# Another order and bank table behind chunk 0's first results in an attention-and-expert kernel

## The chip, the cores and the metric

The kernel runs on one core of one Trainium2 chip. The metric is the device time of one execution in microseconds; the time before is the median of three runs. A profile of one more execution shows what each engine did: TensorE (PE, with its weight loads as PEld), VectorE (DVE), ScalarE (ACT), GpSimd (POOL), SyncE (SP, which only issues DMAs here) and the 16 DMA engines.

## What is computed

```python
# attention: 8 batches, 8 heads, 576 positions, head size 64
kv  = einsum('bhsd,bhse->bhde', k, v)
out = einsum('bhsd,bhde->bhse', q, kv)
rms = sqrt(mean(out * out, axis=-1) + 1e-06)
x   = out / rms * g_norm                  # to 4608 tokens x 512
# expert layer: 512 -> 1024 -> 512
h    = x @ w_in
solu = h * softmax(h)
ln   = (solu - mean(solu)) / sqrt(var(solu) + 1e-06) * g_ln
y    = ln @ w_out
```

Inputs and output are float32; matmuls run in bfloat16.

## The kernel before

The 4608 tokens are taken in nine chunks of 512. Chunks 0 to 7 are the first 512 positions of one batch each; chunk 8 holds the 64 positions that are left of every batch. For each chunk c:

- `q.c`, `k.c`, `v.c` are loads (GpSimd's DMA queue). `kv_mm.c` makes k^T v on TensorE and `kv.c.*` copies it out of PSUM. `qT.c` turns q, for chunks 0 to 4 on TensorE (`qT_mm`, then a copy), for chunks 5 to 8 by a DMA transpose from SP (line 432).
- `o_mm.c` is q times kv. `sq`, `s_mm`, `ln`, `ex`, `x` make the root mean square over a head and scale. For chunks 6 to 8 the tokens lie on the partitions: `sq` on ScalarE, `ssum` on GpSimd, `sred` on VectorE, `rh` on ScalarE, `rg` on GpSimd, `xt` on VectorE, and `x.c` is a DMA transpose from SP (line 507).
- `h.c.*` is x times w_in (lines 590 and 619), in groups of four matmuls of 512 columns. `exp` or `expt` (ScalarE) and `u` or `ut` (VectorE) make h exp(h). For chunks 0 to 3 `usq` and `es` (GpSimd, some of `usq` on ScalarE) and `sums.c` (TensorE) make the statistics, for chunks 4 to 8 `bn` and `stats` on VectorE (lines 639 and 644 to 650). `rstd.c` (ScalarE) makes the factor.
- For chunks 4 to 8 `turnu.c.0` and `turnu.c.1` are DMA transposes from SP (line 655) that turn u for tokens 0 to 255 and 256 to 511 of the chunk.
- `out.c.m` is u times w_out for 128 tokens (line 767), in parts of four matmuls of 512 columns. `out.8.3` is done in two halves of eight matmuls of 256 columns. `ob.c.m` scales it (VectorE or ScalarE) and `store.c.m` writes it out, from SP, or from ScalarE where the table says `:act`. A store of chunk 6 is two DMAs of 64 rows, from SP; chunk 7's stores are eight pieces of 64 rows, half of them (`store.7.m.0`) on SP and half on ScalarE.

There is no scheduler. Each of these steps is a piece of the `Plan`, with the steps that it needs and the buffers that it uses, and a table written out in the file, `ORDER`, names every piece once. `emit` goes through the table and issues piece by piece, so the table is the order of each engine's instructions, of each DMA queue, and of the rotation of buffers (u has two, the scaled outputs of chunks 3 to 8 take turns in four of k's and four of v's buffers, by m even or odd). A word with `:act` or `:dve` behind it puts the piece on that engine. A second table, `HOME`, gives each PSUM tile one of eight banks. A bank is taken over when everything that used its last tile is done, so a piece also waits for those.

On SP the pieces go out one behind the other: a DMA whose input is late holds all that stand behind it. The end of SP's order before is `turnu.7.1 turnu.7.0 store.6.2 store.5.0 store.6.0 turnu.8.1 store.6.1 turnu.8.0 store.6.3 store.7.3.0 store.7.2.0 store.7.0.0 store.7.1.0 store.8.1 store.8.3.1`.

Of the kernel before, what the change touches and what calls it, by code (L numbers as in the profile page):

```python
# [39 lines left out]
store.0.3 qT_mm.3.1 out.0.1.2 qT.3.0 out.0.1.3 h.2.0.0 ex.2.1.1 usq.1.4:act h.2.2.0 h.2.6.0 x.2.1.1 h.2.0.1 kv.3.1.2  # L40
usq.1.0:act kv.3.0.1 ob.0.1 kv.3.0.2 h.2.2.1 exp.2.0 kv.3.1.0:act u.2.0 store.0.0 usq.2.0 h.2.7.0 h.2.7.1 exp.2.2
h.2.5.0 u.2.2 qT.3.1:act exp.2.7 u.2.7 h.2.5.1 exp.2.5 u.2.5 kv_mm.5.0 kv.5.1.0 kv.5.1.1 o_mm.3.1 sq.3.1.0 h.2.6.1
store.0.1 h.2.1.0 kv.5.1.2 h.2.3.0 sq.3.1.1 kv.5.0.2 exp.2.6 u.2.6 h.2.1.1 exp.2.1 v.7.0 k.7.0 s_mm.3.1.1 ln.3.1.1
# [6 lines left out]
sq.4.1.0 ln.4.1.1 store.1.2 es.2.0 kv.6.1.1 es.2.1 qT.5 ex.4.1.1 h.3.4.1 exp.3.4 s_mm.4.1.0 x.4.1.1 h.3.6.1 exp.3.6  # L50
ln.4.1.0 u.3.6 usq.3.6 u.3.4 ex.4.1.0 h.3.5.1 exp.3.5 h.3.1.1 o_mm.4.0 kv_mm.7.0 exp.3.1 x.4.1.0 kv.7.0.0 h.3.7.1
sq.4.0.0 u.3.1 u.3.5 exp.3.7 h.3.2.1 u.3.7 exp.3.2 u.3.2 usq.2.3:act out.2.0.0 kv.7.0.2:act kv.7.0.1 h.3.0.1 exp.3.0
u.3.0 usq.2.5 kv.7.1.1 usq.3.1 s_mm.4.0.0 sq.4.0.1 es.3.3 store.1.3 h.3.3.1 exp.3.3 u.3.3 q_last.1:act out.2.0.1
kv.7.1.2 ln.4.0.0 sums.2 turn.2 store.1.0 kv.7.1.0:act ex.4.0.0 x.4.0.0 s_mm.4.0.1 q.6.0 ln.4.0.1 ex.4.0.1 out.2.2.0
out.2.2.1 stats.2 rstd.2 ob.2.0 o_mm.5.0 sq.5.0.1 ob.2.2 es.3.2 q_last.4 x.4.0.1 o_mm.5.1 sq.5.0.0 qT.6 sq.5.1.1
out.2.3.0 s_mm.5.0.1 ln.5.0.1 out.2.3.1 ob.2.3 usq.3.0 s_mm.5.0.0 q_last.2 s_mm.5.1.1 out.2.1.0 out.2.1.1 ob.2.1
usq.3.4 ln.5.0.0 ex.5.0.1 h.4.2.1 ln.5.1.1 q_last.5 ex.5.0.0 x.5.0.0 usq.3.7 sq.5.1.0 expt.4.2.1 x.5.0.1 h.4.2.0
h.4.1.1 s_mm.5.1.0 ut.4.2.1 h.4.3.1 expt.4.2.0 ut.4.2.0 expt.4.1.1 ut.4.1.1 ex.5.1.1 h.4.3.0 es.3.0 usq.3.2 usq.3.3
x.5.1.1 usq.3.5 es.3.1 sums.3 o_mm.6.1 expt.4.3.1 ut.4.3.1 o_mm.6.0 turn.3 stats.3 expt.4.3.0 ut.4.3.0 ln.5.1.0
ex.5.1.0 x.5.1.0 sq.6.3 h.4.0.0 expt.4.0.0 q.7.0 qT.7 ut.4.0.0 bn.4.1.1 bn.4.3.1 store.2.3 out.3.0.0 out.3.0.1  # L60
q_last.3 h.4.1.0 sq.6.0 sq.6.2 ssum.6.0 sred.6.0 rstd.3 sq.6.1 ssum.6.1 ob.3.0:act store.2.2 expt.4.1.0 ut.4.1.0
bn.4.2.1 sred.6.1 out.3.3.0 out.3.3.1 ob.3.3:act bn.4.0.0 rh.6.0 rg.6.2 rg.6.0 out.3.2.0 out.3.2.1 bn.4.3.0 xt.6.2
turnu.4.1 ob.3.2:act h.4.0.1 h.5.3.0 expt.4.0.1 q_last.6:act rh.6.1 rg.6.1 expt.5.3.0 bn.4.2.0 ut.4.0.1 bn.4.0.1
xt.6.0 out.3.1.0 out.3.1.1 xt.6.1 ut.5.3.0 rg.6.3 xt.6.3 ob.3.1:act o_mm.7.1 store.3.1 sq.7.3 sq.7.1 h.5.2.1 h.5.1.1
expt.5.2.1 ut.5.2.1 expt.5.1.1 ut.5.1.1 h.5.2.0 expt.5.2.0 ut.5.2.0 o_mm.7.0 sq.7.2 bn.4.1.0 stats.4 sq.7.0 h.5.0.0
turnu.4.0 h.5.1.0 expt.5.0.0 ut.5.0.0 ssum.7.1 sred.7.1 h.5.0.1 expt.5.0.1 ut.5.0.1 out.4.2.0 expt.5.1.0 rh.7.1
ut.5.1.0 bn.5.1.0 out.4.2.1 ssum.7.0 rg.7.1 xt.7.1 h.5.3.1 bn.5.3.0 expt.5.3.1 sred.7.0 ut.5.3.1 q_last.7 bn.5.0.0 x.6
qT.8 out.4.1.0 bn.5.3.1 rstd.4 ob.4.2:act out.4.1.1 ob.4.1:act bn.5.2.1 turnu.5.1 rh.7.0 h.6.1.0 turnu.5.0 expt.6.1.0
store.2.1 ut.6.1.0 h.6.2.0 rg.7.3 xt.7.3 h.6.0.1 expt.6.0.1 ut.6.0.1 h.6.2.1 expt.6.2.1 out.4.0.0 out.4.0.1 rg.7.2
expt.6.2.0 o_mm.8.0 sq.8.2 sq.8.0 ut.6.2.0 store.3.3 rg.7.0 xt.7.0 h.6.1.1 xt.7.2 x.7 h.6.3.0 expt.6.1.1 bn.5.1.1  # L70
ut.6.1.1 bn.5.0.1 store.2.0 ssum.8.0 sred.8.0 out.4.3.0 out.4.3.1 expt.6.3.0 store.3.2 ut.6.3.0 ob.4.0:act store.4.0
ob.4.3:act ut.6.2.1 bn.5.2.0 stats.5 rh.8.0 o_mm.8.1 sq.8.3 h.6.0.0 sq.8.1 store.4.1 rg.8.0 xt.8.0 bn.6.1.1 ssum.8.1
sred.8.1 h.6.3.1 store.3.0 out.5.1.0 expt.6.3.1 expt.6.0.0 ut.6.0.0 out.5.3.0 out.5.3.1 rh.8.1 rg.8.3 bn.6.1.0 xt.8.3
rg.8.1 store.4.2 rstd.5 ob.5.3:act store.5.3 out.5.1.1 xt.8.1 h.7.0.0 expt.7.0.0 h.7.1.0 ob.5.1:act h.7.2.1 ut.6.3.1
store.4.3 turnu.6.1 expt.7.1.0 rg.8.2 xt.8.2 bn.6.3.1 store.5.1 x.8 h.7.0.1 expt.7.0.1 bn.6.2.0 bn.6.0.0 ut.7.0.0
ut.7.1.0 h.7.2.0 expt.7.2.0 ut.7.2.0 out.5.0.0 h.7.3.0 expt.7.3.0 out.5.0.1 h.7.3.1 ob.5.0:act expt.7.3.1 turnu.6.0
out.5.2.0 out.5.2.1 bn.7.2.0 bn.6.3.0 h.7.1.1 expt.7.2.1 out.6.2.0 out.6.2.1 ob.5.2:act store.5.2 expt.7.1.1 h.8.3.1
bn.6.2.1 ut.7.3.1 h.8.1.0 bn.6.0.1 stats.6 rstd.6 ut.7.1.1 bn.7.1.1 ut.7.3.0 ut.7.0.1 bn.7.0.1 ut.7.2.1 turnu.7.1
h.8.1.1 expt.8.1.1 bn.7.3.0 expt.8.3.1 ut.8.3.1 h.8.0.0 expt.8.0.0 ut.8.0.0 turnu.7.0 h.8.2.0 expt.8.2.0 h.8.2.1
# [804 lines left out]
```

## Time and profile before

| | |
|---|---|
| median of three runs | 182.72 us (182.57 to 182.72) |
| the profiled execution | 182.41 us |
| its span, first to last instruction | 180.6 us |
| PE, DVE, ACT, POOL busy | 170.4, 135.0, 133.6, 98.6 us |
| DMA | 37.07 MB, mean 205 GB/s |

Rows of a group of instructions read: line, engine, operation, out<-in, shapes, count, busy time. Rows of the chain of waits and of the timeline begin with the start and the length in us; a timeline row ends with the idle time before it and what ended it. A row of waits reads: who <- for whom, us in total, times, the longest. SPq, ACTq and POOLq are the queues that issue DMAs. A DMA's row on its queue shows how long issuing it took, not the transfer.

### The profile page before, as it was taken

The numbers are of one execution on the slowest core, as the hardware profiler recorded it, in microseconds if no ns is written. First come the engines' busy times: TensorE is split into PE (matmuls) and PEld (weight loads), VectorE is DVE, ScalarE is ACT, GpSimd is POOL, SyncE is SP. The second block draws the span as 40 slices with busy tenths as digits, with TensorE's granted clock in tenths as the row PEclk, the third lists the DMA queues.
The fourth block names the chain that finished last, engine by engine and source line by source line (L and its number), as shares of the span: only waits on it lengthen the run. The fifth ranks groups of instructions, "written<-read, shape, count | busy, mean of one in ns | idle before, by whom it ended". The sixth has DMA issues, their size and how long they took to land.

```text
span 180.6 us, 5089 instructions
## 1 busy us (share of the span) xinstructions
PE 170.4 (94%) x2059; PEld 83.7 (46%) x2076; DVE 135.0 (75%) x282; ACT 133.6 (74%) x274; POOL 98.6 (55%) x113
## 2 busy tenths in 40 slices
...
GB/s 187 288 218 208 208 301 338 207 209 207 211 205 253 240 228 208 207 232 161 128 94 131 129 96 237 214 123 155 232 259 289 221 223 134 168 210 164 196 293 198
DMA packets 55996, 37.07 MB, mean 205 GB/s; under 512 B 37404, under 2 KB 49188, under 8 KB 55972
## 3 DMA queue, kind: packets, MB, share of 16 engines
...
q14 instruction: 8, 0.07, 0.1%
HBM read 32.51 MB, written 9.44 MB: 232 GB/s over the span
## 4 chain that ended last, share of the span: by engine, by line
PE 76%; DMA 8%; ACT 7%; DVE 5%; issue 2%; POOL 1%; DVEq 0%; ACTq 0%; POOLq 0%
PE out_ps L767 31%; PE h_ps L619 19%; PE h_ps L590 12%; DMA v_sb<-in_v_dram 5%; PE misc_ps L701 3%; ACT e_sb L597 3%; PE s_ps L515 3%; DMA w_sb<-u_sb 2%; PE misc_ps L385 2%; PE o_ps L451 2%; ACT osq_sb L236 2%; DVE x_sb L535 2%; PE misc_ps L423 2%; DVE u_sb L601 1%; PE o_ps L465 1%
## 5 line engine op out<-in xcount | busy, mean ns | idle before, releaser
L767 PE MATMUL out_ps<-w_out_sb,w_sb 128*128 128x512 bf16 (+1 forms) x166 | 36.4, 369 | 1.6 <-DMA w_sb<-u_sb 1.5
L619 PE MATMUL h_ps<-w_in_sb,x_sb 128*128 128x512 bf16 x153 | 37.0, 379 | 0.4
L238 POOL TENSOR_TENSOR usq_sb<-u_sb 128x512 bf16<-128x512 bf16 x29 | 29.8, 1040 | 12.0 <-DVE u_sb L601 11.9
L627 ACT ACTIVATE e_sb<-h_ps,zero_t 128x512 f32<-128x512 f32 x40 | 27.2, 686 | 5.7 <-PE h_ps L619 5.1
L590 PE MATMUL h_ps<-x_sb,w_in_sb 128*128 128x512 bf16 x128 | 30.6, 379 | 0.8 <-DVE x_sb L535 0.8
L767 PE MATMUL out_ps<-w_out_sb,u_sb 128*128 128x512 bf16 x120 | 29.7, 379 | 0.9 <-issue 0.5
L633 DVE TENSOR_TENSOR u_sb<-h_ps,e_sb 128x512 bf16<-128x512 f32 x40 | 26.3, 680 | 2.2 <-ACT e_sb L627 2.2
L601 DVE TENSOR_TENSOR u_sb<-h_ps,e_sb 128x512 bf16<-128x512 f32 x32 | 20.9, 685 | 7.9 <-ACT e_sb L597 7.7
L639 DVE BATCH_NORM_STATS2 bn_sb<-u_sb 128x6 f32<-128x512 bf16 x40 | 26.0, 681 | 0.2
L767 PEld LDWEIGHTS <-w_sb 128*128 128x128 bf16 x168 | 16.3, 98 | 20.2 <-DMA w_sb<-u_sb 2.3
L535 DVE SCALAR_TENSOR_TENSOR x_sb<-o_ps,g_cols,rst_sb 128x512 bf16<-128x512 f32 x24 | 18.8, 794 | 7.2 <-ACT rst_sb L523 4.0
L597 ACT ACTIVATE e_sb<-h_ps,zero_t 128x512 f32<-128x512 f32 x32 | 20.6, 700 | 4.0 <-PE h_ps L590 3.7
L619 PEld LDWEIGHTS <-x_sb 128*128 128x128 bf16 x160 | 15.0, 98 | 18.3 <-DMA x_sb<-usq_sb 0.5
L614 POOL TENSOR_TENSOR es_sb<-e_sb 128x512 bf16<-128x512 f32 x16 | 20.2, 1274 | 0.0
L590 PEld LDWEIGHTS <-w_in_sb 128*128 128x128 bf16 x128 | 12.1, 98 | 15.6 <-issue 2.4
L236 ACT ACTIVATE osq_sb<-o_ps,zero_t 128x512 bf16<-128x512 f32 x24 | 15.4, 685 | 4.7 <-PE o_ps L451 4.7
L767 PEld LDWEIGHTS <-u_sb 128*128 128x128 bf16 x128 | 12.1, 98 | 14.0 <-issue 1.0
L496 POOL TENSOR_TENSOR lss_sb<-rh_sb,g_all 128x512 f32<-128x512 f32 x12 | 12.4, 1042 | 9.6 <-ACT rh_sb L492 6.6
L519 ACT ACTIVATE lss_sb<-s_ps,eps_t 128x512 f32<-128x512 f32 x20 | 13.9, 694 | 1.6 <-PE s_ps L515 1.5
L523 ACT ACTIVATE rst_sb<-lss_sb,zero_t 128x512 f32<-128x512 f32 x20 | 14.3, 719 | 0.5
L242 ACT ACTIVATE k_sb<-out_ps,rstd_sb 128x512 f32<-128x512 f32 x11 | 7.5, 687 | 7.7 <-PE out_ps L767 7.6
L232 DVE CAST kvd<-misc_ps 64x128 bf16<-64x128 f32 (+1 forms) x29 | 8.1, 286 | 6.8 <-PE misc_ps L385 6.1
...
## 6 DMA issues: line engine op xcount, KB each, us to landing
...
```

Of the source, the lines that this page charges most:

```text
L236: nc.scalar.activation(out=dst, in_=src, func=AF.Square, bias=zero_t[:, :])
L238: on[engine].tensor_tensor(out=dst, in0=src, in1=src, op=MUL)
L535: nc.vector.scalar_tensor_tensor(out=t[:, z, 2 * hf:2 * hf + 2].rearrange("p a (vt w) -> p w (a vt)", w=2), in0=T["o", c, hf, z].rearrange ...
L590: nc.tensor.matmul(bank(("h", c, f), [128, 512])[:, :], w_in_sb[:, dt, f * 128:(f + 1) * 128], T["x", c][:, :, dt, :], start=(dt == 0), st ...
L597: nc.scalar.activation(out=t[:, f % 2, :], in_=T["h", c, f][:, :], func=AF.Exp, bias=zero_t[:, :])
L601: nc.vector.tensor_tensor(out=t[:, f, :], in0=T["h", c, f][:, :], in1=T["e", c, f // 2][:, f % 2, :], op=MUL)
L614: on[engine].tensor_tensor(out=t[:, n, :], in0=e[:, 0, :], in1=e[:, 1, :], op=ADD)
L619: nc.tensor.matmul(bank(("h", c, m, g), [128, 512])[:, :], x[:, NP * (m ^ 2 * odd(c, dt)) + dt, :] if c in TOKA else x[:, m // 2 ^ odd(c, ...
L627: nc.scalar.activation(out=t[:, g, :], in_=T["h", c, m, g][:, :], func=AF.Exp, bias=zero_t[:, :], accum_out=se[:, m, g:g + 1])
L633: nc.vector.tensor_tensor(out=t[:, m, g * 512:(g + 1) * 512], in0=T["h", c, m, g][:, :], in1=T["e", c, m][:, g, :], op=MUL)
L639: nc.vector.bn_stats(out=t[:, m, g, :], in_=T["u", c][:, m, g * 512:(g + 1) * 512])
L767: nc.tensor.matmul(bank(key, [128, d_model])[:, cols], T["w", c][:, m, f, :] if c in TOKS else T["u", c][:, f, m * 128:(m + 1) * 128], w_o ...
```

## The change

Both tables are written anew from one place on. `ORDER` is the same for its first 218 words, up to `out.0.2.2`; behind it all pieces follow in another order, and some copies, scales and squares change between VectorE, ScalarE and GpSimd. `HOME` gives other banks to most tiles from chunk 2 on. No function is changed, no piece is added or left out, and the file is one line shorter. The first lines that differ, two stretches of the middle, and the end:

```diff
-kv.2.0.2:act out.0.3.0 out.0.3.1 out.0.2.1 out.0.2.2 u.1.3 usq.1.3 o_mm.2.0 sq.2.0.1 sq.2.0.0 sums.0 s_mm.2.0.1
...
-h.2.3.1 u.2.1 kv.5.0.0:act h.2.4.0 h.2.4.1 kv.5.0.1 exp.2.3 u.2.3 s_mm.3.1.0 usq.1.6 sums.1 turn.1 usq.2.6 stats.1
-out.1.3.0 exp.2.4 u.2.4 usq.2.4 ln.3.1.0 ex.3.1.0 q.5.0 x.3.1.0 ex.3.1.1 o_mm.3.0 sq.3.0.1 sq.3.0.0 kv_mm.4.0 kv.4.0.1
...
-ob.6.0:act out.6.3.1 ob.6.3:act ut.8.2.1 ut.8.2.0 store.6.2 expt.8.1.0 ut.8.1.1 bn.7.2.1 h.8.0.1 expt.8.0.1 bn.7.0.0
-store.5.0 bn.7.3.1 out.7.1.0 bn.7.1.0 store.6.0 out.7.3.0 ut.8.1.0 out.7.0.0 out.7.3.1 out.7.2.0 out.7.0.1 bn.8.1.1
-turnu.8.1 out.7.2.1 ob.6.1:act store.6.1 stats.7 out.7.1.1 rstd.7 ob.7.2:act ob.7.0:act ob.7.1:act ut.8.0.1 out.8.2.0
-out.8.2.1 bn.8.2.1 turnu.8.0 out.8.1.0 store.7.1.1 store.7.2.1 bn.8.2.0 store.6.3 out.8.1.1 out.8.0.0 out.8.0.1
-bn.8.3.0 ob.7.3 store.7.3.0 bn.8.1.0 bn.8.0.0 bn.8.0.1 stats.8 out.8.3.1 rstd.8 store.7.2.0 store.7.3.1 store.7.0.1
-out.8.3.0 ob.8.2 store.8.2:act ob.8.0:act store.8.0:act store.7.0.0 store.7.1.0 ob.8.1 store.8.1 ob.8.3.0:act
-store.8.3.0:act ob.8.3.1 store.8.3.1
+kv.2.0.2:act out.0.3.0 out.0.3.1 out.0.2.1 out.0.2.2 o_mm.2.0 sq.2.0.0 sums.0 turn.0 stats.0 s_mm.2.0.0 u.1.3 sq.2.0.1
...
+es.2.2 exp.2.2 es.2.1 u.2.2 o_mm.3.1 sq.3.1.1 kv_mm.4.0 kv.4.1.2 kv.4.0.0 h.2.7.0 usq.2.1:act s_mm.3.1.1 ln.3.1.1
...
+out.3.3.0 out.3.3.1 ob.3.0:act ssum.6.1 sred.6.1 rh.6.1 rg.6.0 xt.6.0 expt.5.2.0 ob.3.1 ob.3.3:act h.5.3.1 expt.5.3.1
+o_mm.7.1 sq.7.1 sq.7.3 rg.6.2 ut.5.2.0 xt.6.2 h.5.2.1 expt.5.2.1 h.5.3.0 rg.6.3 xt.6.3 ut.5.3.1 rg.6.1 bn.4.1.0 xt.6.1
+expt.5.3.0 h.5.0.0 expt.5.0.0 h.5.1.0 turnu.4.1 ut.5.2.1 ssum.7.1 h.5.0.1 expt.5.0.1 store.3.2 bn.5.3.1 ut.5.3.0
+sred.7.1 ut.5.0.0 x.6 rh.7.1 o_mm.7.0 ut.5.0.1 out.4.1.0 bn.5.2.0 out.4.2.0 stats.4 out.4.2.1 rg.7.1 bn.5.0.0 h.5.1.1
...
+bn.7.3.0 ut.7.0.0 ut.7.2.1 rstd.6 h.7.1.1 h.7.0.1 h.8.3.1 ut.7.3.1 bn.7.3.1 turnu.7.1 expt.7.1.1 ut.7.1.1 expt.7.0.1
+ut.7.0.1 store.4.0 ut.7.1.0 h.8.2.1 expt.8.3.1 ut.8.3.1 h.8.1.0 expt.8.1.0 ut.8.1.0 h.8.3.0 expt.8.3.0 out.6.0.0
+out.6.0.1 out.6.3.0 turnu.7.0 out.6.3.1 bn.7.0.1 ob.6.0:act store.6.0 h.8.1.1 ob.6.3 store.6.3 ut.8.3.0 bn.7.2.1
+expt.8.2.1 ut.8.2.1 bn.8.2.1 expt.8.1.1 ut.8.1.1 bn.7.2.0 h.8.2.0 expt.8.2.0 out.6.1.0 out.6.1.1 out.6.2.0 out.6.2.1
+h.8.0.0 h.8.0.1 ob.5.1:act store.5.1 out.7.1.0 bn.7.1.1 ut.8.2.0 bn.8.1.1 ob.6.1:act store.6.1 expt.8.0.0 expt.8.0.1
+bn.7.0.0 turnu.8.1 out.7.2.0 ut.8.0.0 out.7.2.1 ut.8.0.1 turnu.8.0 bn.7.1.0 bn.8.3.0 out.7.3.0 out.7.3.1 ob.6.2:act
+stats.7 rstd.7 ob.7.3:act bn.8.0.0 out.7.1.1 ob.7.1:act ob.7.2 store.7.2.0 store.7.1.1 store.6.2 store.7.3.0 out.7.0.0
+out.7.0.1 ob.7.0:act store.7.0.1 out.8.1.0 bn.8.2.0 store.7.0.0 store.7.2.1 out.8.1.1 bn.8.1.0 bn.8.3.1 store.7.1.0
+bn.8.0.1 stats.8 store.7.3.1 rstd.8 ob.8.1:act out.8.0.0 out.8.0.1 ob.8.0 store.8.0:act out.8.2.0 out.8.2.1 ob.8.2:act
+store.8.2:act out.8.3.1 ob.8.3.1 out.8.3.0 ob.8.3.0:act store.8.1 store.8.3.0:act store.8.3.1
```

SP's order after it ends `turnu.6.0 turnu.6.1 x.8 store.5.0 store.4.3 store.5.3 store.5.2 turnu.7.1 store.4.0 turnu.7.0 store.6.0 store.6.3 store.5.1 store.6.1 turnu.8.1 turnu.8.0 store.7.2.0 store.6.2 store.7.3.0 store.7.0.0 store.7.1.0 store.8.1 store.8.3.1`. Before, the same stretch began `turnu.6.1 store.5.1 x.8 turnu.6.0 store.5.2`.

More of the change, by code (lines that the diff above doesn't have):

```diff
@@ L40 @@
[L40 to L43, printed above, removed]
-h.2.3.1 u.2.1 kv.5.0.0:act h.2.4.0 h.2.4.1 kv.5.0.1 exp.2.3 u.2.3 s_mm.3.1.0 usq.1.6 sums.1 turn.1 usq.2.6 stats.1
@@ L50 @@
[L50 to L79, printed above, removed]
@@ new lines @@
+ob.0.3 out.0.2.3 ob.0.2 usq.1.4 o_mm.2.1 sq.2.1.0 out.0.0.1 out.0.0.2 out.0.0.3 ob.0.0 v.6.0 s_mm.2.1.0 sq.2.1.1
+out.0.1.0 ln.2.1.0 kv_mm.3.0 ex.2.1.0 x.2.1.0 es.1.2 kv.3.1.2:act s_mm.2.1.1 ln.2.1.1 ex.2.1.1 out.0.1.1 out.0.1.2
+kv.3.1.1 out.0.1.3 ob.0.1:act usq.1.0 usq.1.1:act x.2.1.1 kv.3.1.0:act store.0.1 h.2.4.0 kv.3.0.2 h.2.3.0 kv.3.0.0
+h.2.0.0 store.0.3 h.2.1.0 h.2.0.1 h.2.6.0 exp.2.0 kv.3.0.1:act h.2.1.1 exp.2.1 u.2.1 h.2.3.1 h.2.4.1 exp.2.3 usq.1.6
+qT_mm.3.1 h.2.6.1 v.7.0 exp.2.6 k.7.0 u.2.0 qT.3.1 kv_mm.5.0 kv.5.0.2 store.0.2 u.2.3 exp.2.4 kv.5.1.0:act
@@ new lines @@
+kv.5.0.1:act kv.5.0.0 es.2.0 u.2.6 kv.5.1.1:act kv.5.1.2 u.2.4 h.2.5.0 h.2.5.1 exp.2.5 usq.1.3 u.2.5 h.2.2.0 h.2.2.1
+es.2.2 exp.2.2 es.2.1 u.2.2 o_mm.3.1 sq.3.1.1 kv_mm.4.0 kv.4.1.2 kv.4.0.0 h.2.7.0 usq.2.1:act s_mm.3.1.1 ln.3.1.1
+ex.3.1.1 x.3.1.1 sq.3.1.0 kv.4.1.1 kv.4.0.2 kv.4.0.1 usq.2.4 h.2.7.1 exp.2.7 out.1.2.0 out.1.2.1 o_mm.3.0 store.0.0
+sq.3.0.1 u.2.7 kv.4.1.0:act q_last.2 usq.2.0:act es.2.3 sums.1 s_mm.3.0.1 out.1.0.0 turn.1 stats.1 qT_mm.4.0 ln.3.0.1
+ex.3.0.1 qT_mm.4.1 q_last.1 qT.4.0 rstd.1 sq.3.0.0 ob.1.2:act out.1.0.1 s_mm.3.1.0 out.1.3.0 s_mm.3.0.0 ob.1.0 qT.4.1
```

66 lines of the change are left out of this document (42 added, 24 removed).

## The prediction

> **What bounds the kernel now.** I read the page first, then the busy time by stage, then the chain that ended last, then the waits of TensorE alone, and last the SP queue around the end.
>
> ```profile
> span 180.6 us, 5089 instructions
> PE 170.4 (94%) x2059; PEld 83.7 (46%) x2076; DVE 135.0 (75%) x282; ACT 133.6 (74%) x274; POOL 98.6 (55%) x113
> ```
>
> ```profile
> 0.00:45.00 45.00, 41.29 (x576) 20.44 (x578) 25.23 (x54) 30.13 (x49) 33.16 (x45) 1.00 1.14 237
> 45.00:105.00 60.00, 59.09 (x1042) 31.09 (x1049) 48.13 (x100) 54.70 (x106) 42.22 (x45) 1.00 0.98 184
> 105.00:125.00 20.00, 19.89 (x151) 9.09 (x152) 18.25 (x37) 17.33 (x45) 14.24 (x16) 1.00 0.94 170
> 125.00:165.00 40.00, 39.79 (x241) 18.02 (x245) 36.84 (x77) 27.82 (x70) 8.95 (x10) 1.00 0.89 211
> 170.00:181.00 11.00, 5.39 (x33) 3.05 (x32) 1.99 (x3) 1.76 (x4) 0.00 (x0) 1.00 0.76 232
> ```
>
> The columns of the second fence are the length, then busy PE, PEld, DVE, ACT, POOL, then clock, DMA share and GB/s. TensorE bounds the program. It is idle 3.7 us in the first 45 us, 0.91 + 0.11 + 0.21 = 1.2 us in the 120 us after that, and 5.2 us from 170 to the end at 180.6. The clock is 1.00 throughout, so the matmuls themselves offer nothing. VectorE is busy 18.25 of 20 and 36.84 of 40 us: behind TensorE, and close.
>
> ```profile
> 161.39 3.47 PE out_ps L767 x16
> ...
> 167.09 4.42 DMA w_sb<-u_sb
> ...
> 171.55 5.39 PE out_ps L767 x32
> ...
> 176.96 0.47 ACT v_sb L242
> ```
>
> ```profile
> PE out_ps L767 <- DMA w_sb<-u_sb: 1.5, 1, 1.5
> PE out_ps L767 <- issue: 0.5, 2, 0.4
> ```
>
> The chain of waits is TensorE work nearly all the way and then one DMA: chunk 8's second transpose (turnu.8.0) is issued at 167.09 and lands 4.42 us later, and TensorE waits 1.5 us for it, the longest single wait there is. Behind it stand out.8.1, out.8.0 and out.8.3 (5.39 us) and the last scale and store. The other row of waits is from the window 45 to 165: 0.5 us in two places. The order is the same up to out.0.2.2 (about 45 us), so the 3.7 us at the start stay. What is to be won is the 1.5 us and at most the 0.5 us.
>
> **Part 1: the end.** Why was turnu.8.0 late?
>
> ```profile
> 152.98 4.42 SPq L655 DMA_TRANSPOSE w_sb<-u_sb  x2
> 157.50 1.70 SPq L783 DMA_DIRECT2D out_dram<-k_sb  x2
> 159.25 0.60 SPq L796 DMA_DIRECT2D out_dram<-k_sb  x1
> 159.94 2.84 SPq L783 DMA_DIRECT2D out_dram<-k_sb  x2
> 162.90 2.10 SPq L655 DMA_TRANSPOSE w_sb<-u_sb  x1
> 165.11 1.87 SPq L783 DMA_DIRECT2D out_dram<-v_sb  x2
> 167.09 2.45 SPq L655 DMA_TRANSPOSE w_sb<-u_sb  x1
> ```
>
> ```profile
> 163.90 0.68 DVE L633 TENSOR_TENSOR u_sb<-h_ps,e_sb 128x512 bf16<-128x512 f32 x1
> 164.50 1.87 DVE L639 BATCH_NORM_STATS2 bn_sb<-u_sb 128x6 f32<-128x512 bf16 x3
> 171.55 5.37 PE L767 MATMUL out_ps<-w_out_sb,w_sb 128*128 128x512 bf16 x32 [1.53 <-DMA w_sb<-u_sb]
> ```
>
> Its last input, ut.8.0.1, was done at 163.90 + 0.68 = 164.58. SP was then inside turnu.8.1 until 165.0 and then issued store.6.1's two half stores, to 167.0. After the change nothing stands between the two transposes. But two other things move. First, out.8.2, eight matmuls, now stands behind out.8.1, so the cover for turnu.8.0 shrinks. A matmul costs 3.47 / 16 = 0.217 us, so TensorE reaches out.8.1 at 171.55 - 1.53 - 8 x 0.217 = 168.3 instead of 170.0. Second, SP has seven issues between turnu.7.0 and turnu.8.1 (both halves of store.6.0, 6.3 and 6.1, and store.5.1) where it had five. The five took 157.50 to 162.78, 1.06 us each. Seven are 7.4 us.
>
> When does turnu.7.0 end? Before, it followed turnu.7.1, to 157.4, and both waited until ten VectorE pieces behind chunk 7's last h were through. In the new order chunk 7's last h stands at the same place of TensorE's order, and five VectorE pieces follow up to turnu.7.0's last input. A piece costs 0.60 us (three bn in 1.87, of which the last has 0.68), so it can be five pieces, 3.0 us, earlier: end 154.4. Then 154.4 + 7.4 = 161.8 for turnu.8.1, which keeps SP 2.2 us (162.90 to 165.11): turnu.8.0 goes out at 164.0 and lands, with 4.42, at 168.4. That is a wait of 0.1, or 0.3 with the median landing below, where there was 1.53. I take a gain of 1.3. The bounds: all of 1.53 if SP is quicker, and a loss of 1.6 if the five VectorE pieces bring nothing (167.0 + 4.42 - 168.3 = 3.1 of wait).
>
> ```profile
> DMA to landing us min/median/max: 4.3/4.6/6.9
> ```
>
> This is the view of the transposes of line 655, issue to landing.
>
> Behind turnu.8.0 on SP stand eight store issues; new among them is store.6.2, whose buffer ob.8.2 needs.
>
> ```profile
> out_dram<-k_sb SPq DMA_DIRECT2D x6, 128.0 KB, 4.2
> ```
>
> turnu.8.0 keeps SP to 166.5, store.7.2.0 and the first half of store.6.2 to 168.6, and with 4.2 the second half lands at 172.8. TensorE ends out.8.2 at 171.55 + 5.39 - 1.3 - 8 x 0.217 = 173.9. Cover 1.1: no cost.
>
> The Trainium skill's page "DMA: Bandwidth & Descriptors", section "Issuing engines are not separate DMA queues", speaks against it: DMAs of all engines interleave on the same 16 DMA engines, and what is saved by the place of issue is sequencer time alone, usually small beside the transfer. Here the trace differs, since the two half stores held SP for 1.98 of the 4.42 us; by the rule the gain of 1.3 would be about nothing and the sum would come out near 183.
>
> **Part 2: what else moves between 45 and 160 us.** The pieces are the same; only order, banks and some engines differ. 17 copies, scales and squares go to ScalarE, 13 to VectorE, 5 to GpSimd; ScalarE and VectorE end with one piece fewer each, GpSimd with two more. I cost this at nothing, since TensorE covers all three engines in the rows by stage; where the cover is gone a piece costs its own duration. The places where it is thin follow.
>
> kv_mm.4 comes earlier: seven pieces that stood ahead of it (h.2.7, two s_mm, sums.1, out.1.3.0, o_mm.3.0) now stand behind.
>
> ```profile
> 63.90 1.23 PE misc_ps L701 x80
> 65.45 0.38 issue
> 66.42 0.34 PE o_ps L451 x8
> 66.77 0.61 PE misc_ps L385 x72
> ```
>
> ```profile
> 43.06 0.76 POOL L325 DMA_DIRECT2D k_sb<-in_k_dram  x1
> DMA to landing us min/median/max: 18.8/18.8/18.8
> ```
>
> They are worth 1.23 (sums.1), 0.34 (o_mm.3.0) and ten matmuls of 0.217, 3.7 us together, so kv_mm.4 is wanted at 66.77 - 3.7 - 0.4 (the idle time ahead of it, which hung on sums.1) = 62.7; k.4, issued at 43.06, landed at 61.9. Chunk 0's four stores compete with that load in both orders, a little later in the new one. Cover 0.8 us; cost nothing, bound 0.9 (one more store ahead of it).
>
> VectorE's long run: u.5 may not be written before out.3 has been read to its end (out.3.3.1). From there to xt.7.1, which frees the bank for h.6.3.0, VectorE has 14 pieces of 0.60, one sred (0.33) and stats.4.
>
> ```profile
> 117.10 0.47 DVE L644 BATCH_NORM_AGGREGATE mv<-bn_sb 128x2 f32<-128x12 f32 x4
> 118.73 0.68 DVE L633 TENSOR_TENSOR u_sb<-h_ps,e_sb 128x512 bf16<-128x512 f32 x1
> 119.33 0.41 DVE L485 TENSOR_REDUCE rh_sb<-es_sb 128x16 f32<-128x256 f32 x1
> 111.69 0.38 PE o_ps L465 x32
> ```
>
> stats.4 took 117.10 to 118.73, 1.63 us; in all 8.4 + 0.33 + 1.63 = 10.4. TensorE has 44 matmuls and two o_mm there: 9.55 + 0.76 = 10.3. So VectorE becomes the bound of this stretch by about 0.1, and by what it may wait. A stall is 0.1 to 0.2 if nothing is late.
>
> x.8 and h.8.3.1: out.6.2, eight matmuls, no longer stands ahead, so x.8 is wanted 1.7 us sooner.
>
> ```profile
> 144.08 2.73 SPq L507 DMA_TRANSPOSE x_sb<-usq_sb  x1
> 140.85 0.68 DVE L503 TENSOR_TENSOR usq_sb<-o_ps,lss_sb 128x512 bf16<-128x512 f32 x1
> 148.92 0.53 PEld L619 LDWEIGHTS <-x_sb 128*128 128x128 bf16 x3
> ```
>
> Before it was issued at 144.08, 2.5 us behind its last input (141.53), because SP had turnu.6.1 and a store ahead. Both are now ahead of it early. Its input can come up to 1.2 us later (o_mm.8.0 stands 1.2 us of TensorE's work further back, o_mm.8.1 3 us further forward); with 0.8 the issue is at 142.4, landing by the 4.6 above 147.0; wanted at 148.9 - 1.7 = 147.2. Cost 0 to 0.3. With the run of VectorE I take 0.3 for both.
>
> **The sum.** -1.3 + 0.3 = -1.0 us. The profiled execution took 182.41 us in all (span 180.6 and 1.8 around it) and would take 181.4; the median of the three runs, 182.72, stands 0.3 above it: 181.7.
>
> **The rivals.** First, on the other side: SP is late with turnu.8.1. The place is the seven issues ahead of it. For it: the last two halves before took 2.84 us, and the cover is 1.7 us shorter, so that any issue of turnu.8.0 after 168.3 + 1.53 - 4.42 = 165.4 is worse than before. Against it: five VectorE pieces fewer. At the bound of part 1: 182.7 + 1.6 + 0.3 = 184.6; half way from the forecast's 0.1 of wait to that bound's 3.1, 183.1.
>
> Second, the neighbours disturb each other: a transpose right behind another lands late. For it: one of the ten took 6.9 us. Against it: the pair at 152.98 went out in 4.42 together. Price 6.9 - 4.42 = 2.5, less what is left of the hole: a wait of 2.6 and 182.7 - 1.53 + 2.6 + 0.3 = 184.1.
>
> Third, VectorE's run waits for GpSimd, whose products it takes in order.
>
> ```profile
> POOL lss_sb L496 <- ACT rh_sb L492: 6.6, 5, 1.7
> DVE rh_sb L485 <- POOL es_sb L480: 1.6, 2, 1.3
> ```
>
> Since the run has no spare time, each wait goes to TensorE in full: with two of the mean of 1.3, 181.7 + 2.6 - 0.3 = 184.0; with one, 182.7.
>
> Fourth, no change: kv_mm.4's 0.9 is paid and the end gains as said: 182.6.
>
> **How the numbers follow.** Two kernels that differ by less than 0.2% (0.37 us) can't be told apart here. Forecast 0.60, with its own range 180.7 (all of 1.53 and the 0.5 of issue) to 182.3; first rival 0.13, second 0.07, third 0.12 (a third of it near no change), fourth 0.08. Faster: 0.57 from the forecast and 0.01 from the fourth, 0.58. Same: 0.02 + 0.04 + 0.05 = 0.11. Slower: the rest, 0.31. The range goes from 180.7 to 184.0, which leaves out the worst ends of the rivals.
>
> **What would show it.** In the changed profile TensorE's wait for w_sb should be under 0.5 us, the two transposes of chunk 8 should be 2.2 to 2.5 us apart on SP with turnu.8.0 issued by 164.3, and 32 matmuls should follow without a gap. TensorE's idle time from 45 to 165 should stay under 1.6. It is wrong if w_sb is still waited for by over 1 us, if a wait of h_ps or out_ps for VectorE of over 0.5 appears near 110 to 122, or if misc_ps waits for k_sb near 62.

## The result: 0.4 to 0.5% slower, and the profile after

The changed kernel took 183.32 us (median of 17 runs, 182.47 to 184.22) where the kernel before took 182.24: a ratio of 1.0054, 95% interval 1.0036 to 1.0073. Measured once more with the last experiments, it took 182.58 against 182.22, a ratio of 1.0043 (1.0018 to 1.0068). So it is slower by 0.3 to 1.3 us; 1.0 us faster was forecast. The profiled execution took 183.55 us. The ratios here and below leave out three executions at a lower clock: two of the six of "stats.4 later", the profiled one among them, and one of the six of "before, small stores".

In its profile every line number is one smaller than before, because the file is a line shorter. First the busy time by stage, with the columns as before:

```profile
45.00:105.00 60.00, 59.07 (x965) 30.69 (x973) 47.25 (x94) 55.60 (x109) 42.71 (x46) 1.00 1.04 195
105.00:125.00 20.00, 18.39 (x216) 8.81 (x218) 18.60 (x40) 14.40 (x37) 13.98 (x15) 1.00 0.80 167
125.00:165.00 40.00, 39.36 (x240) 17.95 (x243) 36.65 (x73) 28.08 (x72) 9.88 (x10) 1.00 0.89 198
```

TensorE's idle time from 45 to 165 us is 0.93 + 1.61 + 0.64 = 3.18 us; before it was 1.23. Of the growth of 1.95 us, 1.50 lies between 105 and 125 us, where TensorE had been idle for 0.11 us, and 0.43 behind that. Now TensorE's own waits of over 0.3 us, from 45 us to the end:

```profile
PE h_ps L618 <- DVE usq_sb L502: 1.1, 1, 1.1
PE h_ps L618 <- DMA x_sb<-usq_sb: 0.5, 1, 0.5
PE misc_ps L700 <- issue: 0.4, 1, 0.4
```

The wait for w_sb (1.5 us before) is no longer in the list; three that were not there before have come in. The third row has no releaser. SP's timeline and the last steps of the chain show how the end closed:

```profile
163.37 5.09 SPq L654 DMA_TRANSPOSE w_sb<-u_sb  x2
...
166.10 2.36 SPq L654 DMA_TRANSPOSE w_sb<-u_sb  x1
```

```profile
165.23 10.74 PE out_ps L766 x49
176.02 2.36 PE out_ps L766 x18
```

Chunk 8's two transposes go out as one row, of which the last line is the second one alone, and TensorE runs without a wait to its end at 178.38. The largest new wait, 1.1 us of `h.6.3.0` for `xt.7.1` (which frees its bank), leads to VectorE's timeline ahead of it, and GpSimd's beside it:

```profile
113.55 0.69 DVE L632 TENSOR_TENSOR u_sb<-h_ps,e_sb 128x512 bf16<-128x512 f32 x1 [0.54 <-PE out_ps L766]
...
121.16 0.41 DVE L643 BATCH_NORM_AGGREGATE mv<-bn_sb 128x2 f32<-128x12 f32 x4
121.48 0.11 DVE L645 TENSOR_TENSOR s<-se_sb 128x4 f32<-128x4 f32 x1
121.62 0.97 DVE L647 SCALAR_TENSOR_TENSOR s<-s 128x4 f32<-128x4 f32 x1
122.62 1.08 DVE L649 TENSOR_TENSOR vare_sb<-mv,s 128x4 f32<-128x4 f32 x1
...
124.23 0.67 DVE L502 TENSOR_TENSOR usq_sb<-o_ps,lss_sb 128x512 bf16<-128x512 f32 x1
```

```profile
120.53 2.04 POOL L495 TENSOR_TENSOR lss_sb<-rh_sb,g_all 128x512 f32<-128x512 f32 x2 [2.21 <-ACT rh_sb L491]
122.53 1.16 POOL L479 TENSOR_TENSOR es_sb<-rst_sb 128x512 f32<-128x512 bf16 x1
```

VectorE works without a pause from 113.55 to 124.90, 11.35 us. In that, two instructions on 128x4 elements, each with two operands in SBUF, take 0.97 and 1.08 us. They end at 122.59 and 123.70; the GpSimd instructions beside them end at 122.57 and 123.69. The first of the two lines over the whole of the same profile (count, then ns as minimum/median/maximum):

```profile
L647 DVE SCALAR_TENSOR_TENSOR s<-s x5: 161/163/966, 121.6 to 172.3; 128x4 f32<-128x4 f32 x5
```

At its four other places, where GpSimd is idle, it takes 0.16 us.

### The profile page after: what moved, and what is told of

It reads as the page before. It is cut to its first block, busy times and chain, and to the rows that moved or that the text cites. A ratio compares the mean times of both kernels' runs of the same rounds, so it can differ in the third digit from the quotient of the medians.

```text
span 181.8 us, 5092 instructions
## 1 busy us (share of the span) xinstructions
PE 172.1 (95%) x2058; PEld 84.6 (47%) x2076; DVE 135.4 (74%) x281; ACT 133.6 (74%) x273; POOL 99.5 (55%) x115
## 4 chain that ended last, share of the span: by engine, by line
PE 63%; DVE 17%; ACT 12%; DMA 3%; issue 3%; ACTq 0%; DVEq 0%
PE out_ps L766 26%; PE h_ps L618 13%; PE h_ps L589 8%; ACT e_sb L596 4%; DVE u_sb L632 4%; DVE u_sb L600 4%; DVE bn_sb L638 3%; DMA x_sb<-usq_sb 3%; PE s_ps L839 3%; ACT osq_sb L235 3%; DVE x_sb L534 2%; PE misc_ps L700 2%; PE misc_ps L422 2%; PE s_ps L514 2%; PE o_ps L839 2%
## 5 line engine op out<-in xcount | busy, mean ns | idle before, releaser
L618 PE MATMUL h_ps<-w_in_sb,x_sb 128*128 128x512 bf16 x157 | 37.5, 379 | 1.7 <-DVE usq_sb L502 1.1
L613 POOL TENSOR_TENSOR es_sb<-e_sb 128x512 bf16<-128x512 f32 x16 | 20.3, 1276 | 13.5 <-issue 10.4
L638 DVE BATCH_NORM_STATS2 bn_sb<-u_sb 128x6 f32<-128x512 bf16 x40 | 26.5, 683 | 0.2
L479 POOL TENSOR_TENSOR es_sb<-rst_sb 128x512 f32<-128x512 bf16 x6 | 7.0, 1159 | 9.5 <-ACT rst_sb L235 9.5
L231 DVE CAST kvd<-misc_ps 64x128 bf16<-64x128 f32 (+1 forms) x24 | 6.6, 287 | 6.6 <-PE misc_ps L384 6.2
```

What stands on the lines that cost most here:

```text
L613: on[engine].tensor_tensor(out=t[:, n, :], in0=e[:, 0, :], in1=e[:, 1, :], op=ADD)
L618: nc.tensor.matmul(bank(("h", c, m, g), [128, 512])[:, :], x[:, NP * (m ^ 2 * odd(c, dt)) + dt, :] if c in TOKA else x[:, m // 2 ^ odd(c, ...
L638: nc.vector.bn_stats(out=t[:, m, g, :], in_=T["u", c][:, m, g * 512:(g + 1) * 512])
```

## The experiments

The ratios below are to the kernel before, measured on the same chip beside each (its median was 182.19 to 182.24 us each time). One per mille is 0.18 us.

| kernel | median of all, us | ratio (95%) | TensorE's waits from 45 us on, without those of 0.3 and less |
|---|---|---|---|
| changed, first measured | 183.32 | 1.0054 (1.0036 to 1.0073) | usq_sb 1.1, x_sb 0.5, misc_ps 0.4 |
| changed, control | 182.58 | 1.0043 (1.0018 to 1.0068) | usq_sb 1.1, x_sb 0.4 |
| changed, stats.4 earlier | 181.69 | 0.9988 (0.9963 to 1.0013) | none |
| changed, one source each | 181.78 | 0.9981 (0.9961 to 1.0001) | x_sb 0.4 |
| changed, stats.4 later | 186.02 | 1.0171 (1.0124 to 1.0219) | out_ps for ScalarE 3.3, misc_ps 0.7 |
| changed, x.7 earlier | 182.58 | 1.0034 (1.0010 to 1.0057) | usq_sb 1.1 |
| changed, one source and x.7 earlier | 180.81 | 0.9937 (0.9914 to 0.9961) | none |
| the same, store.6.1 between the transposes | 182.29 | 1.0016 (0.9995 to 1.0038) | w_sb 1.0, misc_ps 0.4 |
| changed, store.6.1 between the transposes | 184.07 | 1.0110 (1.0084 to 1.0136) | usq_sb 1.1, w_sb 0.8, x_sb 0.5, misc_ps 0.4 |
| before, only the end changed | 181.96 | 0.9992 (0.9968 to 1.0015) | 0.4 of issue in two |
| before, one source each | 181.71 | 0.9983 (0.9956 to 1.0010) | w_sb 1.0, issue 0.5 in two |
| before, small stores | 180.70 | 0.9919 (0.9894 to 0.9945) | w_sb 0.7, issue 0.4 in two |
| before, end changed, small stores | 180.99 | 0.9932 (0.9906 to 0.9958) | none |

### The control

No edit.

> The changed kernel itself, as the control of these runs: 183.0 to 183.6 us, with waits of 1.1 (h_ps for usq_sb), 0.5 (x_sb) and 0.4 us (in the sums of chunk 3) in its profile. If the waits differ from those by over 0.2 us, they are not a property of the order.

182.58 us is below the foreseen 183.0 to 183.6. Its waits for usq_sb and x_sb, 1.1 and 0.4 us, belong to the order. The wait in chunk 3's sums (misc_ps) is 0.2 here and 0.4 there. The windows of the control:

```profile
45.00:105.00 60.00, 59.11 (x1017) 30.99 (x1028) 47.23 (x93) 55.83 (x107) 42.09 (x46) 1.00 1.02 197
105.00:125.00 20.00, 18.63 (x180) 8.67 (x172) 18.83 (x41) 14.63 (x39) 13.43 (x15) 1.00 0.79 161
125.00:165.00 40.00, 39.39 (x241) 17.97 (x243) 36.56 (x73) 27.59 (x70) 9.85 (x10) 1.00 0.92 206
```

The idle time by stage is the same within 0.3 us. The two executions differ by 1.5 us all the same, and most of it comes ahead of the place where the tables part. The first `h` matmuls of chunk 0, a step that all kernels here share, as the chain has them in the kernel before, in the first changed execution and in the control:

```profile
20.30 1.02 PE h_ps L590 x4
...
20.90 1.02 PE h_ps L589 x4
...
19.81 1.02 PE h_ps L590 x4
```

From there TensorE takes 156.64 us to its end before (at 176.94), 157.48 in the first changed execution (178.38) and 157.10 in the control (176.91). By this the new order costs 0.5 to 0.8 us in these executions, and what an execution wins or loses ahead of it is no property of the order.

### stats.4 earlier

```diff
-sred.7.1 ut.5.0.0 x.6 rh.7.1 o_mm.7.0 ut.5.0.1 out.4.1.0 bn.5.2.0 out.4.2.0 stats.4 out.4.2.1
+sred.7.1 stats.4 ut.5.0.0 x.6 rh.7.1 o_mm.7.0 ut.5.0.1 out.4.1.0 bn.5.2.0 out.4.2.0 out.4.2.1
```

> The changed kernel with stats.4 moved five VectorE pieces forward, to right behind sred.7.1; its instructions keep their form. In the changed kernel's profile GpSimd is idle from 118.32 to 120.53 and sred.7.1 ends at 119.3. Theory (the 2.5 us of stats.4 are a hold by GpSimd's running instruction, so they shrink wherever GpSimd is idle): stats.4 takes 0.8 to 1.0 us, the wait of h_ps for usq_sb of 1.1 us falls to under 0.3, the time falls by 0.8 to 1.5 us below the changed kernel's in these runs. Rival (the instructions are slow in themselves, or it is the number of pieces ahead of xt.7.1 that counts): stats.4 stays near 2.5 us and the time within 0.3 us.

The timelines of VectorE and GpSimd in that kernel:

```profile
118.28 0.41 DVE L644 BATCH_NORM_AGGREGATE mv<-bn_sb 128x2 f32<-128x12 f32 x4
118.61 0.11 DVE L646 TENSOR_TENSOR s<-se_sb 128x4 f32<-128x4 f32 x1
118.75 0.16 DVE L648 SCALAR_TENSOR_TENSOR s<-s 128x4 f32<-128x4 f32 x1
118.95 0.16 DVE L650 TENSOR_TENSOR vare_sb<-mv,s 128x4 f32<-128x4 f32 x1
```

```profile
116.61 0.73 POOL L480 TENSOR_TENSOR es_sb<-es_sb 128x256 f32<-128x256 f32 x1
119.55 2.04 POOL L496 TENSOR_TENSOR lss_sb<-rh_sb,g_all 128x512 f32<-128x512 f32 x2 [2.21 <-ACT rh_sb L492]
```

(It passes three of VectorE's pieces; the expectation miscounts them as five.) The same instructions, with as many pieces ahead of xt.7.1 as before, in a stretch where GpSimd is idle: 118.28 to 119.11, 0.83 us instead of 2.54. The wait for usq_sb is gone. The time fell by 0.0055 of the kernel before, 1.0 us. This is the theory's outcome in each number. The wait for x_sb is gone too, which the theory does not say; x.7 still left SP behind the same transposes and stores, and why it was not late here is not shown.

### One source each

(The tile mv also gets a third column, for the square.)

```diff
-nc.vector.tensor_tensor(out=s[:, :], in0=T["se", c][:, :, 0], in1=T["se", c][:, :, 1], op=ADD)
+nc.vector.tensor_reduce(out=s[:, :], in_=T["se", c][:, :, :], op=ADD, axis=mybir.AxisListType.X)
...
-nc.vector.scalar_tensor_tensor(out=s2[:, :], in0=s[:, :], scalar=1e-6, in1=s[:, :], op0=MUL, op1=MUL)
+for m in range(4):
+    nc.vector.tensor_scalar(out=mv[:, m, 2:3], in0=s[:, m:m + 1], scalar1=s[:, m:m + 1], scalar2=1e-6, op0=MUL, op1=MUL)
...
-nc.vector.tensor_tensor(out=vare[:, :], in0=mv[:, :, 1], in1=s2[:, :], op=ADD)
+nc.vector.tensor_reduce(out=vare[:, :], in_=mv[:, :, 1:3], op=ADD, axis=mybir.AxisListType.X)
```

> The changed kernel with the sum, the square and the last sum of the row statistics of chunks 4 to 8 written so that no VectorE instruction reads two SBUF tensors (a reduction over the pair, four products by a scalar per partition, a reduction over the pair). The order stays. Theory (these small instructions wait until GpSimd's running tensor instruction ends, since both read SBUF through one interface): stats.4 shrinks from 2.47 to 0.9 to 1.3 us, the wait of h_ps for usq_sb falls from 1.1 to under 0.3, and the time by 0.7 to 1.1 us. Rival (they were slow for another reason, such as waiting for bn_sb or the clock of the records): stats.4 stays above 2 us and the time within 0.3 us.

In its profile GpSimd works beside stats.4 as in the changed kernel:

```profile
119.79 0.41 DVE L644 BATCH_NORM_AGGREGATE mv<-bn_sb 128x2 f32<-128x12 f32 x4
120.11 0.11 DVE L646 TENSOR_REDUCE s<-se_sb 128x4 f32<-128x8 f32 x1
120.25 0.57 DVE L648 TENSOR_SCALAR mv<-s 128x1 f32<-128x1 f32 x4
120.86 0.16 DVE L650 TENSOR_REDUCE vare_sb<-mv 128x4 f32<-128x8 f32 x1
...
121.54 0.67 DVE L503 TENSOR_TENSOR usq_sb<-o_ps,lss_sb 128x512 bf16<-128x512 f32 x1
```

```profile
119.16 2.04 POOL L496 TENSOR_TENSOR lss_sb<-rh_sb,g_all 128x512 f32<-128x512 f32 x2 [2.21 <-ACT rh_sb L492]
121.16 1.16 POOL L480 TENSOR_TENSOR es_sb<-rst_sb 128x512 f32<-128x512 bf16 x1
```

GpSimd is busy from 119.16 to 122.32 and nothing is held: stats.4 takes 1.23 us. (The last line of VectorE's is xt.7.1.) The gain is 0.0062 to 0.0073 of the kernel before, 1.1 to 1.3 us. So the place and the form of stats.4 each remove the hold, one without the other.

### One source each, in the kernel before

The same edit.

> The kernel before with the row statistics of chunks 4 to 8 written with one SBUF tensor per VectorE instruction, order unchanged. In the kernel before the same instructions were held by GpSimd too (0.51 and 0.59 us instead of 0.11 to 0.16), but TensorE did not wait for VectorE there. Theory (the hold is paid only where VectorE's run has no cover): within 0.3 us of the kernel before, 181.9 to 182.5. Rival (the new form is faster by itself, wherever it stands, which would make the 1.5 us of the changed kernel say little about its order): 0.5 us or more below the kernel before.

The ratio, 0.9983, has 1 in its interval, and 0.5 us of gain too; it excludes neither theory. Its profile has no wait for VectorE to lose, and its w_sb wait is 1.0 instead of 1.5. What can be said is that the edit is worth at most 0.8 us there.

### stats.4 later

```diff
-out.4.2.0 stats.4 out.4.2.1 rg.7.1
+out.4.2.0 out.4.2.1 rg.7.1
...
-xt.7.3 rstd.4
+xt.7.3 stats.4 rstd.4
```

> The changed kernel with stats.4 (its eight small VectorE instructions) moved behind xt.7.1 and xt.7.3, just ahead of rstd.4. Theory (VectorE's run from out.3.3.1 to xt.7.1 is the bound of that stretch, and stats.4's 2.5 us in it are what TensorE waits for): xt.7.1 ends 2.3 to 2.5 us earlier, the wait of h_ps for usq_sb of 1.1 us goes, and the time falls by 0.8 to 1.3 us against the changed kernel (182.0 to 182.5). Rival (something else holds h.6.3.0, or the 1.1 us comes back at the next wait, x.7's 0.5): less than 0.4 us gained, or the wait for x_sb grows to 1.5.

A miss: the ratio rose to 1.0171, 2.1 to 2.3 us above the changed kernel, where 0.8 to 1.3 us of gain was foreseen. The wait for usq_sb did go, but another came, as TensorE's timeline and VectorE's show:

```profile
129.51 1.56 PE L767 MATMUL out_ps<-w_out_sb,w_sb 128*128 128x512 bf16 x4 [3.34 <-ACT v_sb L242]
```

```profile
125.06 0.42 DVE L485 TENSOR_REDUCE rh_sb<-es_sb 128x16 f32<-128x256 f32 x1 [0.90 <-POOL es_sb L480]
...
126.00 0.41 DVE L644 BATCH_NORM_AGGREGATE mv<-bn_sb 128x2 f32<-128x12 f32 x4
```

sred.7.0, now ahead of stats.4, waits 0.9 us for GpSimd; stats.4 starts at 126.00, and the scaling of out.4.2 and out.4.1, which needs its result, frees their banks 3.3 us after out.4.3 wanted one. This profile's clock is lower only behind that wait (0.67 from 130 to 135 us, 1.00 up to 125), so the wait is not made by it. Of the two places tried, only the earlier one pays.

### x.7 earlier

```diff
-store.4.1 rg.8.0 xt.8.0 rstd.5 rh.8.1 rg.8.3 ob.5.0:act bn.6.2.0 store.2.3 out.5.3.1 x.7
+rg.8.0 xt.8.0 rstd.5 rh.8.1 rg.8.3 ob.5.0:act bn.6.2.0 out.5.3.1 x.7 store.4.1 store.2.3
```

> The changed kernel with store.4.1 and store.2.3 moved behind x.7, nothing else. Theory (x.7's lateness of 0.5 us is a cost of its own beside stats.4's 1.1): the wait of h_ps for x_sb goes, the one for usq_sb stays at 1.0 to 1.2, the time falls by 0.3 to 0.7 us below the changed kernel's in these runs. Rival (both waits are one: whatever stats.4 makes late is late for x.7 too): less than 0.2 us.

SP's timeline of the changed kernel, and of this one, from the end of two transposes (at 132.87 and 132.48) to x.7:

```profile
132.96 0.70 SPq L795 DMA_DIRECT2D out_dram<-v_sb  x1
133.72 0.59 SPq L795 DMA_DIRECT2D out_dram<-ob_sb  x1
134.41 3.57 SPq L506 DMA_TRANSPOSE x_sb<-usq_sb  x1
```

```profile
132.58 2.29 SPq L507 DMA_TRANSPOSE x_sb<-usq_sb  x1
```

The wait for x_sb went and the one for usq_sb stayed at 1.1, as the theory has it. The time did not show it: 1.0034 against the control's 1.0043, with intervals wider than the 0.3 to 0.7 us that were sought.

The same edit on top of the one-source statistics:

> The changed kernel with the one-source row statistics and with store.4.1 and store.2.3 moved behind x.7 on SP. Theory (x.7, ready at 131.25 and issued at 134.41 behind two transposes and two stores, is 0.4 to 0.6 us late for h.7.2.1): x.7 leaves 1.4 us earlier in the stream, the wait of h_ps for x_sb goes, and the time falls by 0.3 to 0.6 us below the one-source kernel's 181.78 (181.1 to 181.5). Rival (the end is set by the stores by then, or the gap comes back at the next transpose): within 0.2 us of 181.78.

Here it showed: from 0.9981 to 0.9937, 0.8 us, a little more than foreseen. At 180.81 us this is the fastest kernel here that writes its whole output, 0.4 to 0.9% below the kernel before.

### The end alone, in the order before

```diff
-turnu.8.1 out.7.2.1 ob.6.1:act store.6.1 stats.7
+turnu.8.1 out.7.2.1 ob.6.1:act stats.7
...
-out.8.2.1 bn.8.2.1 turnu.8.0 out.8.1.0
+out.8.2.1 bn.8.2.1 turnu.8.0 store.6.1 out.8.1.0
```

> The kernel before with one edit: chunk 6's second half store (store.6.1, two issues of 1.0 us on SP) stands behind turnu.8.0 instead of between chunk 8's two transposes; nothing else moves, out.8.2 still covers turnu.8.0. Theory (the tail gain is real and stands by itself; what the whole change lost, it lost earlier): turnu.8.0 is issued at 165.1 instead of 167.1, lands at 169.5, TensorE reaches out.8.1 at 170.0, the wait of 1.53 us for w_sb is gone: 1.3 to 1.6 us below the kernel before. Rival (the place on SP saves sequencer time only, or the next wait takes over): within 0.4 us of the kernel before.

The wait of 1.5 us went, but the time did not follow: 181.96 us, ratio 0.9992. TensorE's last step:

```profile
165.50 10.13 PE out_ps L767 x54
```

TensorE is done at 175.63, 1.3 us earlier than before, and the span, 180.7 us, ends where it ended before: 5.1 us later, where it had been 3.7. The last stretches of the windows, in the kernel before, then in this one:

```profile
174.00:177.00 3.00, 2.92 (x22) 1.90 (x20) 0.73 (x2) 0.72 (x2) 0.00 (x0) 1.00 0.95 324
177.00:180.00 3.00, 0.00 (x0) 0.00 (x0) 0.00 (x0) 0.44 (x1) 0.00 (x0) 1.00 0.50 183
```

```profile
174.00:177.00 3.00, 1.61 (x15) 1.19 (x13) 0.48 (x1) 1.16 (x2) 0.00 (x0) 1.00 0.97 318
177.00:180.00 3.00, 0.00 (x0) 0.00 (x0) 0.00 (x0) 0.00 (x0) 0.00 (x0) 1.00 0.54 197
```

The last column but one: from 174 to 177 us the DMA engines are all but full in both, and then half busy. TensorE has moved and the stores have not.

To test it, store.6.1 and store.6.3 write 4 rows instead of 64 per half, in both kernels, so that 0.5 MB of the output is left out:

```diff
-rows = out[c * S:c * S + S, :].rearrange("(p j) d -> p j d", j=9)
-on[engine].dma_start(rows[:, 4 * (m % 2) + m // 2 + 2 * x, :], T[ob_key(c, m)][64 * x:64 * x + 64, :])
+rows, n = out[c * S:c * S + S, :].rearrange("(p j) d -> p j d", j=9), 4 if (c, m) in ((6, 1), (6, 3)) else 64
+on[engine].dma_start(rows[0:n, 4 * (m % 2) + m // 2 + 2 * x, :], T[ob_key(c, m)][64 * x:64 * x + n, :])
```

> The kernel with only store.6.1 moved behind turnu.8.0, and the same 0.5 MB of output left out (store.6.1 and store.6.3 write 4 rows instead of 64 each). Theory (there the end is set by the output still draining through the DMA engines, 98% busy from 165 to 179 us, and not by TensorE, which is 1.3 us earlier): 0.5 MB at 380 GB/s is 1.3 us, so the time falls by 0.8 to 1.3 us against the same kernel with full stores, to 180.7 to 181.2. Rival (something else holds the end, such as the fixed time of the last store): within 0.3 us of it, 181.7 to 182.3.

The kernel with the end changed fell from 0.9992 to 0.9932, 1.1 us, as foreseen, and its last stretch now reads:

```profile
177.00:180.00 3.00, 0.00 (x0) 0.00 (x0) 0.00 (x0) 0.00 (x0) 0.00 (x0) 1.00 0.16 57
```

With full stores and with small ones it has no wait for w_sb, so here the output held the end.

> The kernel before, with the half stores of chunk 6's blocks 1 and 3 (store.6.1, store.6.3) writing 4 rows each instead of 64: 0.5 MB of the output is left out, the instructions and their order stay. It is the control of the next run. Theory (the end of the kernel before is set by TensorE, with the wait of 1.5 us in it): within 0.5 us of the kernel before, unless SP's issues of the small stores get shorter and turnu.8.0 leaves earlier (up to 1 us).

The control is not a clean one. It fell by 1.5 us, more than allowed for: its small stores were issued faster and the wait for w_sb shrank to 0.7, and what is left of the fall would be the drain in the kernel before, too. How the two share it is open. Nor is the kernel with the end changed the faster one of the two with small stores (0.9932 against 0.9919, with intervals that overlap): that the closed hole pays once there is less output is not shown.

### The end undone, in the changed order

```diff
-turnu.8.1 out.7.2.0 ut.8.0.0 out.7.2.1 ut.8.0.1 turnu.8.0
+turnu.8.1 store.6.1 out.7.2.0 ut.8.0.0 out.7.2.1 ut.8.0.1 turnu.8.0
```

(store.6.1 leaves its place ahead of turnu.8.1.)

> The changed kernel with store.6.1 put back between turnu.8.1 and turnu.8.0. Theory A (in the changed order turnu.8.0 waits for its last input, ready at 166.07, not for SP; what closed the hole is the later TensorE, not that the transposes are neighbours): turnu.8.0 still leaves by 166.4, no wait for w_sb above 0.3 us, time within 0.4 us of the changed kernel (183.0 to 183.7). Theory B (being neighbours closed it): turnu.8.0 leaves 1.1 to 2.0 us later, w_sb is waited for by 0.5 to 1.4 us, time 183.8 to 184.7.

Theory A fell. SP's timeline of this kernel:

```profile
162.93 1.88 SPq L655 DMA_TRANSPOSE w_sb<-u_sb  x1
164.90 1.68 SPq L783 DMA_DIRECT2D out_dram<-v_sb  x2
166.68 2.29 SPq L655 DMA_TRANSPOSE w_sb<-u_sb  x1
```

The transposes start 3.75 us apart instead of 2.7, w_sb is waited for by 0.8 us, and the ratio rises by 0.0056 to 0.0067, 1.0 to 1.2 us. The same edit on the fastest kernel, where no other wait stands ahead:

> The fastest kernel so far (changed order, one-source row statistics, x.7 ahead of two stores) with store.6.1 put back between turnu.8.1 and turnu.8.0, that is, the named part of the change undone where nothing else is late. There turnu.8.0 leaves at 163.9 and lands 4.3 us later, and TensorE reaches out.8.1 at 168.6, 0.4 us behind the landing. Theory (the two half stores keep SP 1.0 to 1.2 us longer, and TensorE sets the end): w_sb is waited for by 0.5 to 0.9 us and the time rises by 0.4 to 0.9 us, to 181.2 to 181.7. Rival (the end is set by the stores there as well, as in the kernel with the tail alone): within 0.2 us of 180.81.

From 0.9937 to 1.0016: 1.4 us, more than the 0.4 to 0.9 foreseen, with 1.0 us of wait for w_sb. Being neighbours is worth 1.0 to 1.4 us in the changed order, with the other waits and without them.

## Why the prediction was wrong

**The end: the mechanism and the size were right, its place in the sum only in part.** "I take a gain of 1.3": the hole closed, and undoing it costs 1.0 to 1.4 us in the changed order. Step by step: turnu.8.1 was to follow seven issues at 161.8 and was issued at 163.37; turnu.8.0, forecast at 164.0, left at 166.10, 2.7 us behind it instead of 2.2. Each left within 0.1 us of its last input (163.30 and 166.07), so SP was not late; the inputs came later, as all of TensorE did, and nothing waited for it. What the step did not ask is what ends second. In the order before, the same edit alone brings 0.15 us (ratio 0.9992, interval to 0.9968, or 0.6 us), where the full DMA engines and the small stores point to output that is still draining. The changed order does not meet that bound: its span ends 3.4 us behind TensorE's last matmul in both executions (181.8 - 178.38 and 180.3 - 176.91), where the end alone left 5.1.

The Trainium skill's page "DMA: Bandwidth & Descriptors", section "Issuing engines are not separate DMA queues", has it that issuing from several engines saves only sequencer time, usually small beside the transfer. Sequencer time is what was saved here too, on one queue, but it was not small: two half stores on SP between the transposes cost 1.0 to 1.4 us.

**VectorE's long run: the step that failed.** "stats.4 took 117.10 to 118.73, 1.63 us; in all 8.4 + 0.33 + 1.63 = 10.4 [...] A stall is 0.1 to 0.2 if nothing is late." The run took 11.35 us, because stats.4 took 2.54, and TensorE waited 1.1. The 1.63 was no price of the work: 0.83 us is (with stats.4 earlier), and the rest of the old row was a hold by GpSimd that happened to be shorter. VectorE and GpSimd in the kernel before:

```profile
117.48 0.51 DVE L646 TENSOR_TENSOR s<-se_sb 128x4 f32<-128x4 f32 x1
118.03 0.16 DVE L648 SCALAR_TENSOR_TENSOR s<-s 128x4 f32<-128x4 f32 x1
118.22 0.59 DVE L650 TENSOR_TENSOR vare_sb<-mv,s 128x4 f32<-128x4 f32 x1
```

```profile
116.82 1.15 POOL L480 TENSOR_TENSOR es_sb<-rst_sb 128x512 f32<-128x512 bf16 x1 [0.83 <-ACT rst_sb L236]
118.05 0.74 POOL L480 TENSOR_TENSOR es_sb<-es_sb 128x256 f32<-128x256 f32 x1
```

The instructions of 0.51 and 0.59 us end at 117.99 and 118.81, 0.02 us behind GpSimd's at 117.97 and 118.79; the one of 0.16 began 0.02 us ahead of GpSimd's second and was not held. In the run without cover the longer hold goes to TensorE in full: a wait of h_ps for VectorE of over 0.5 us, one of the prediction's own signs of being wrong. The place and the direction had been read rightly (VectorE becomes the bound there by about 0.1); the term was short by 0.9. With it the forecast change of -1.0 becomes -0.1, and the measured one is +0.3 to +1.3: x.7 and chunk 3's sums, below, were left out as well. (As a time it makes 182.6, beside the control's 182.58 by luck: the forecast counted from 182.72, and the kernel before took 182.22 to 182.24.)

**The third rival came nearest.** It was VectorE's run waiting for GpSimd, 182.7 with one wait and 184.0 with two, at a chance of 0.12. But it named waits for GpSimd's products. In the changed kernel the products were in time; what VectorE waited for was the end of GpSimd's instruction, which the waits for lss_sb and es_sb do not show.

**x.7 was left out.** The prediction followed x.8 on SP's queue and put 0.3 on it together with VectorE's run; it did not follow x.7, which stood behind two transposes and two stores and came 0.4 to 0.5 us late. x.8 was not waited for.

**kv_mm.4 cost nothing**, as said: no wait of misc_ps for k_sb appears, so the fourth rival is out. None of TensorE's waits with a known releaser is for one of the 35 copies, squares and scales that changed engines, as assumed.

**The balance.** TensorE lost 3.18 - 1.23 = 1.95 us between 45 and 165 (2.87 - 1.23 = 1.64 in the control), and won the hole of 1.53. That makes 0.1 to 0.4 us slower, where the profiles have 0.5 to 0.8 from chunk 0's first h on. The difference lies inside TensorE's busy time, 152.92 us from that step on before and 153.28 in both changed executions; in which instructions is not shown, and neither is a releaser of the 0.2 to 0.4 us in chunk 3's sums.
